# Rows of a convolution kernel: four row bands of TensorE at once, evicted by ScalarE and turned by the store

## The chip, the cores and the metric

The kernel runs on one core of one Trainium2 chip. A core has five engines with instruction queues of their own: TensorE (PE in the profile; its weight loads are shown apart, as PEld), VectorE (DVE), ScalarE (ACT), GpSimd (POOL) and SyncE (SP), which issues most DMAs. The metric is the time of one execution on the device in microseconds; the median of the runs counts.

## The reference

Four layers act on x of 2048 rows by 512 columns (S and D). Layer A filters a normalised x in the two-dimensional frequency domain; layer B convolves each column of a normalised x with a kernel of its own, as long as the sequence, made from a state space of 128 complex states per column. Each adds its result to x, in the order A, B, A, B, with the same weights in both rounds.

```python
def _A_ref(x, w_r, w_i):
    X = rfft2(x, axes=(-2, -1)) * (w_r + 1j * w_i)
    return irfft2(X, s=(S, D), axes=(-2, -1))

def _B_ref(u, A_re, A_im, B_re, B_im, C_re, C_im, log_dt, Dskip):
    dt = exp(log_dt)[:, None]
    logdA, dB = dt * (A_re + 1j * A_im), dt * (B_re + 1j * B_im)
    P = exp(logdA[:, :, None] * arange(L)[None, None, :])
    K = einsum("dn,dnl,dn->dl", C_re + 1j * C_im, P, dB).real
    y = irfft2(rfft2(pad(u.T)) * rfft2(pad(K)))[..., :L]     # along the sequence
    return y.T + u * Dskip

x = x + _A_ref(layernorm(x), ...)
x = x + _B_ref(layernorm(x), ...)
x = x + _A_ref(layernorm(x), ...)
x = x + _B_ref(layernorm(x), ...)
```

What the change touches is on the way from the parameters to the spectrum of K, layer B's kernel. K does not depend on x, is worked out once and serves both rounds.

## The kernel before, in words

**Stages.** The program has four stages: layer A together with all the work on K; layer B; layer A again; layer B again. The Fourier transforms are matmuls with tables, in two steps each, in 32-bit floats.

**K in the first stage.** K is built in eight batches b of 64 columns. Of a batch, six evictions with Exp (exp_k, L1013) and four units (unit_k: L1027 to L1068) make the powers of the states and multiply them out; the unit's matmuls are L1059, their result is copied to a tile KS by L1068. Then rows_k (L1071) takes the first step of K's transform. On the 128 partitions of KS lie four bands of 32 rows, each with 16 of the batch's 64 columns. A matmul of a band takes 32 rows of the table Rk as weights (32 x 128) and 32 rows of KS as the moving side (512 elements), into one PSUM bank of all 128 partitions; a band needs two that add up (h = 0, 1). So there are eight matmuls a batch, each of them two records in the profile, which appear as L1086 with the tile 32*128. Two bands (j = 0, 1) share a PSUM tile of two banks; a = 0, 1 counts these pairs. After each pair's four matmuls DVE empties the tile with a transpose in blocks of 32x32 (L1090) into half of the tile T, and after both SP stores T, 128 rows of 8 KB, to the scratch yk in DRAM (L1093).

**Who reads yk.** In the second stage step_b loads pieces of yk (L813), after all eight batches are stored; L797 multiplies them with the table Gb, ScalarE copies the spectrum out (L819) and it is kept in DRAM as khat for the last stage. The tables Gb and Ib (L769, L770) lie where T and other tiles of the first stage were, so they are loaded after the last store of T has finished; on SP the loads of yk stand behind them. Also needed is layer B's own input: the normalised x (norm_b, L502), its rows (forward_b, matmul L786 and DVE's transpose L789).

**Beside it in the first stage** run layer A's pieces: forward_a (L543 to L551), first_a (fold L564, L664 to L705, with DVE at L673 to L681), inv_a (matmuls L721 and L730, copies L725 and L733, POOL L738 to L746, DVE L741 to L751, and the statistics L479 and L480 for the next norm).

**The order of the work.** A list scheduler in the kernel (Clock) writes the program out while it is built. Every piece of work is a generator; each `yield` names the engines, tiles and PSUM tiles that the next step needs. The scheduler holds a clock for each engine and a price list (fixed part, price per element) and takes, among the steps that can start soonest, the one of lowest rank. rows_k has rank 0. The price of a matmul depends on the shape of its weights. Each engine then executes its instructions in the order written.

**Tiles.** Work tiles come from rings of fixed places: T has one place, KS two, the tables of first_a (G) five. PSUM tiles of kind a, each two banks, are three; the Exp evictions, the units, first_a and rows_k share them.

Of the kernel before, what the change touches and what calls it, by code (L numbers as in the profile page):

```python
# [169 lines left out]
class Clock:  # L170
# [81 lines left out]
    def note(self, ready):  # L252
# [3 lines left out]
        for ins in listed[self.n:]:  # L256
# [7 lines left out]
            start = self.free.get(engine, 0.0)  # L264
            for name, box, w in boxes:
                for other, t, v, by in self.seen.get(name, ()):
                    if (w or v) and t > start and (w != v or box[0][2] > 1) and engine != by and self.meet(box, other):
                        start = t
            out = ins.outs[0].bass_ap
            n = max(int(np.prod([b for _, b in a.ap[1:]])) for a, _ in aps)  # L270
            fixed, each, hop = COST[engine]
# [5 lines left out]
            else:  # L277
                if engine == "PE":
                    n = int(np.prod([b for _, b in out.ap[1:]]))
                    stat, rows = aps[1][0], out.ap[0][1]  # L280
                    if aps[0][0].dtype == BF:
                        each *= 0.25
                    elif rows < 128 and stat.ap[0][1] < 128:
                        each *= max(rows, 32) * stat.ap[0][1] / 16384
                    elif rows < 128:
                        fixed, each = fixed + (0.015 if rows > 32 else -0.005), each * max(rows, 32) / 128
                    elif stat.ap[0][1] < 128:
                        fixed, each = fixed + 0.03, each * max(stat.ap[0][1], 64) / 128
                    elif stat.ap[-1][0] > 2:
                        each *= 2  # L290
                    form = rows, stat.ap[0][1]
# [6 lines left out]
                elif engine == "DVE":  # L298
# [3 lines left out]
                    if ins.opcode == "Reciprocal":  # L302
                        each = 6.3
# [74 lines left out]
class Net:  # L378
# [692 lines left out]
    def rows_k(self, b, KS):  # L1071

        nc = self.nc
        yield "POOL", self.after("kernel", 4 * b + 4)
        o = KS[b][:, 1, :, 0]
        nc.gpsimd.tensor_tensor(o, o, self.Dk[:, 16 * b:16 * b + 16], op=OP.add)
        K = KS[b].rearrange("p h d s -> p h (d s)")
        for a in range(2):
            yield "PE p:a" if a else "PE p:a T"
            if a == 0:  # L1080
                T = self.w("T", [128, 32, 64])
            p = self.psum("a")
            for h in range(2):
                for j in range(2):
                    o = slice(64 * a + 32 * j, 64 * a + 32 * j + 32)
                    nc.tensor.matmul(p[:, 512 * j:512 * j + 512], self.Rk[o, h, :], K[o, h, :], start=h == 0, stop=h == 1)  # L1086
            if a:
                self.drop(KS[b])
            yield "DVE"
            nc.vector.transpose(T[:, :, 32 * a:32 * a + 32].rearrange("p k d -> p d k"), p.rearrange("p (d s) -> p d s", s=32))  # L1090
            self.drop(p)
        yield "SP"
        nc.sync.dma_start(self.yk[b], T.rearrange("p k d -> p (k d)"))  # L1093
        self.mark("rows_k")

    def plan_k(self):
# [173 lines left out]
```

## Time and profile before

Three runs took 852.89 us (median), 852.57 and 856.74. The profiled execution is one of its own:

| | |
|---|---|
| profiled execution | 864.48 us |
| its span, first to last instruction | 862.7 us |
| mean granted clock of TensorE | 0.873 |
| instructions | 20721 |
| busy: PE, PEld | 611.4 us (71%), 369.6 us (43%) |
| busy: DVE, ACT, POOL | 629.9 us (73%), 416.0 us (48%), 361.5 us (42%) |
| L1086, first and last start | 122.0 and 381.2 us |
| first matmul of layer B (L786), first on yk (L797) | 392.36 and 406.72 us |
| DMA | 40132 packets, 82.02 MB, mean 95 GB/s |

Busy time of an engine is a mean over stages that have different limits; the prediction's table of stretches divides it. In a row of a group stand line, engine, operation, tiles, shapes and count, then busy time and the mean ns of one, then the idle time of the engine just before these instructions and what ended it. In a row of a timeline stand start, length, engine, line, operation, shapes and count, and in brackets the wait. Matmuls overlap, so the length of a group of matmuls says more than that of one.

### The profile page before, as it was taken

The numbers are of one execution on the slowest core, as the hardware profiler recorded it, in microseconds if no ns is written. First come the engines' busy times: TensorE is split into PE (matmuls) and PEld (weight loads), VectorE is DVE, ScalarE is ACT, GpSimd is POOL, SyncE is SP. The second block draws the span as 40 slices with busy tenths as digits, with TensorE's granted clock in tenths as the row PEclk, the third lists the DMA queues.
The fourth block names the chain that finished last, engine by engine and source line by source line (L and its number), as shares of the span: only waits on it lengthen the run. The fifth ranks groups of instructions, "written<-read, shape, count | busy, mean of one in ns | idle before, by whom it ended". The sixth has DMA issues, their size and how long they took to land. (4 is left out here: it accounts for less than half of the span.)

```text
span 862.7 us, 20721 instructions
## 1 busy us (share of the span) xinstructions
PE 611.4 (71%) x8808; PEld 369.6 (43%) x8808; DVE 629.9 (73%) x894; ACT 416.0 (48%) x721; POOL 361.5 (42%) x331
## 2 busy tenths in 40 slices
PE   0048689888999778656887874398787863787843
PEld 0037445656667434321444330297675431343410
DVE  6988776965868888976555847776755897756863
ACT  1447686877677866651333330284442553132310
POOL 0037742734537557730334230283432772343510
PEclk9999778999999969857999976599987996997975
DMA  9434003323230601015554312303540003232325
GB/s 235 118 127 122 13 14 130 104 81 104 81 122 26 199 35 51 2 50 206 205 178 149 124 51 80 121 2 127 197 148 1 3 1 146 75 100 75 59 41 97
DMA packets 40132, 82.02 MB, mean 95 GB/s; under 512 B 3465, under 2 KB 21257, under 8 KB 38633
## 3 DMA queue, kind: packets, MB, share of 16 engines
q1 hardware_dynamic: 37736, 72.32, 27.0%
q10 hardware_dynamic: 2304, 8.39, 2.4%
q8 instruction: 69, 1.13, 0.6%
q14 instruction: 23, 0.18, 0.1%
HBM read 57.75 MB, written 22.94 MB: 94 GB/s over the span
## 5 line engine op out<-in xcount | busy, mean ns | idle before, releaser
L837 POOL TENSOR_TENSOR wk<-wk 128x1024 f32<-128x1024 f32 x32 | 75.6, 2366 | 164.0 <-ACT wk L833 164.0
L1046 POOL TENSOR_TENSOR Y<-wk,Y 128x1024 f32<-128x1024 f32 x32 | 77.0, 2407 | 49.7 <-ACT wk L1032 27.7
L845 PE MATMUL ps<-wk 32*64 32x256 f32 x2048 | 76.2, 412 | 18.8 <-POOL wk L837 11.3
L543 PE MATMUL ps<-cRa,wk 128*128 128x128 f32 x128 | 27.7, 301 | 65.7 <-POOL wk L528 65.7
L528 POOL TENSOR_TENSOR wk<-wk 128x256 f32<-128x256 f32 x32 | 25.4, 795 | 101.0 <-DVE wk L504 55.3
L845 PEld LDWEIGHTS ps<-wk 32*64 32x64 f32 x2048 | 43.9, 139 | 53.3 <-POOL wk L837 19.8
L830 DVE TENSOR_TENSOR wk<-ps,wk 128x1024 f32<-128x1024 f32 x32 | 39.0, 1229 | 28.0 <-PE ps L797 18.8
L833 ACT COPY wk<-ps 128x512 f32<-128x512 f32 x32 | 18.8, 586 | 81.6 <-DVE wk L830 81.6
L789 DVE STREAM_TRANSPOSE Y<-ps 128x1024 f32<-128x1024 f32 x24 | 43.6, 1902 | 16.1 <-PE ps L786 16.1
L997 PE MATMUL ps<-wk,Y 96*128 96x512 bf16 x128 | 44.5, 425 | 14.4 <-DVE Y L1040 10.0
L1090 DVE STREAM_TRANSPOSE wk<-ps 128x1024 f32<-128x1024 f32 x16 | 31.6, 1973 | 31.1 <-PE ps L1086 13.8
L1059 PE MATMUL ps<-Y 128*32 128x64 f32 x2048 | 42.3, 245 | 15.0 <-POOL Y L1047 5.7
L1029 DVE SCALAR_TENSOR_TENSOR wk<-wk,ps 128x1024 f32<-128x1024 f32 x32 | 38.8, 1212 | 17.3 <-ACT wk L1027 17.1
L543 PEld LDWEIGHTS ps<-cRa,wk 128*128 128x128 f32 x128 | 21.8, 211 | 68.5 <-POOL wk L528 67.6
L1013 ACT ACTIVATE Y<-ps 128x1024 f32<-128x1024 f32 x48 | 46.7, 1040 | 7.4 <-PE ps L997 7.3
L730 PE MATMUL ps<-wk,cRaT 128*128 128x512 f32 x64 | 38.9, 700 | 15.4 <-ACT wk L725 10.1
L1059 PEld LDWEIGHTS ps<-Y 128*32 128x32 f32 x2048 | 37.0, 126 | 24.8 <-POOL Y L1047 13.1
L1040 DVE TENSOR_TENSOR Y<-ps,Y 128x1024 f32<-128x1024 f32 x32 | 38.9, 1216 | 7.6 <-ACT ps L1033 7.3
L851 ACT COPY Y<-ps 128x512 f32<-128x512 f32 x48 | 25.8, 591 | 36.3 <-PE ps L845 36.3
L862 DVE STREAM_TRANSPOSE Ya<-Y 128x1024 f32<-128x1024 f32 x16 | 35.9, 2267 | 9.9 <-ACT Y L851 9.9
L1047 POOL TENSOR_TENSOR Y<-wk,Y 128x512 f32<-128x512 f32 x32 | 42.4, 1324 | 0.0
L1032 ACT ACTIVATE wk<-wk,quarter 128x1024 f32<-128x1024 f32 x32 | 36.7, 1148 | 10.8 <-DVE wk L1030 10.6
(222 smaller groups left out, 1765.3 us busy)
## 6 DMA issues: line engine op xcount, KB each, us to landing
yk<-wk SPq DMA_DIRECT2D x8, 1024.0 KB
wk<-yk SPq DMA_DIRECT2D x16, 512.0 KB
khat<-wk ACTq DMA_DIRECT2D x16, 512.0 KB
wk<-khat SPq DMA_DIRECT2D x16, 512.0 KB
Y<-in_W_dram SPq DMA_DIRECT2D x12, 515.0 KB
x<-in_cPa_dram SPq DMA_DIRECT2D x16, 384.0 KB
Y<-in_cGa_dram SPq DMA_DIRECT2D x12, 384.0 KB
x<-in_W_dram SPq DMA_DIRECT2D x16, 258.0 KB
```

The costliest lines, as they stand in the source:

```text
L543: nc.tensor.matmul(o, pq[:, 0, :], self.Ra, start=True, stop=False)
L730: nc.tensor.matmul(q, self.RaT, Y4, start=True, stop=True)
L789: nc.vector.transpose(self.P[r][e][:, :, o:o + 32].rearrange("p k d -> p d k"), p.rearrange("p (s d) -> p d s", s=32))
L830: nc.vector.tensor_tensor(t0, X[:, :, 0, None, :].to_broadcast(four), kh, op=OP.mult)
L837: nc.gpsimd.tensor_tensor(t1, xi[:, :, None, :].to_broadcast(four), kh[:, :, ::-1, :], op=OP.mult)
L845: nc.tensor.matmul(v[i // 2][64 * a:64 * a + 64, 512 * (i % 2):512 * (i % 2) + 256], self.Ib[o, g, a, b, :], t[o, a, c, :], start=n == 0, ...
L997: self.nc.tensor.matmul(p, f[:, c:c + 128], self.oh[:k, o:o + 512], start=True, stop=True)
L1013: nc.scalar.activation(m[:, :, 1024:] if i == 2 else m[:, i, :1024], p.rearrange("p (i m) -> p i m", i=2) if i == 2 else p, AF.Exp)
L1040: nc.vector.tensor_tensor(E[:, 1, :1024], p, m[:, :1024], op=OP.mult)
L1046: nc.gpsimd.tensor_tensor(E[:, 0, :1024], c, m[:, :1024], op=OP.mult)
L1047: nc.gpsimd.tensor_tensor(rows(E[:, 0, 1024:]), back(c[:, 512:]), rows(m[:, 1024:]), op=OP.mult)
L1059: nc.tensor.matmul(pk[32 * j:32 * j + 32, 64 * e:64 * e + 64], E1[:, r, i, :], E2[:, r, i], start=r == 0, stop=r == 1)
```

## The change

rows_k issues all eight matmuls of a batch in one step, with the four bands side by side: it takes two PSUM tiles of kind a at once, four banks, and goes through the four bands for h = 0 and then for h = 1. The two tiles are emptied by ScalarE copies and not by DVE's transposes; a copy reads PSUM with a step of 32 elements, so that T holds, on partition k of a block of 32, the elements s by d where the transpose put partition s with k by d. The store takes over the exchange of k and s: four DMAs, each for a block of 32 partitions, which write pieces of 64 elements (256 bytes). The scratch yk has the same contents as before. In the scheduler's price list the price of a matmul with fewer than 128 weight rows and 128 columns changes: a smaller fixed part, and a price that falls down to 32 rows and not only to 64.

```diff
--- before.py
+++ after.py
@@ -285,7 +285,7 @@
                     elif rows < 128:
                         fixed, each = fixed + (0.015 if rows > 32 else -0.005), each * max(rows, 32) / 128
                     elif stat.ap[0][1] < 128:
-                        fixed, each = fixed + 0.03, each * max(stat.ap[0][1], 64) / 128
+                        fixed, each = fixed + 0.01, each * max(stat.ap[0][1], 32) / 128
                     elif stat.ap[-1][0] > 2:
                         each *= 2
                     form = rows, stat.ap[0][1]
@@ -1075,22 +1075,22 @@
         o = KS[b][:, 1, :, 0]
         nc.gpsimd.tensor_tensor(o, o, self.Dk[:, 16 * b:16 * b + 16], op=OP.add)
         K = KS[b].rearrange("p h d s -> p h (d s)")
-        for a in range(2):
-            yield "PE p:a" if a else "PE p:a T"
-            if a == 0:
-                T = self.w("T", [128, 32, 64])
-            p = self.psum("a")
-            for h in range(2):
+        yield "PE p:a p:a T"
+        T = self.w("T", [128, 32, 64])
+        ps = [self.psum("a") for _ in range(2)]
+        for h in range(2):
+            for a in range(2):
                 for j in range(2):
                     o = slice(64 * a + 32 * j, 64 * a + 32 * j + 32)
-                    nc.tensor.matmul(p[:, 512 * j:512 * j + 512], self.Rk[o, h, :], K[o, h, :], start=h == 0, stop=h == 1)
-            if a:
-                self.drop(KS[b])
-            yield "DVE"
-            nc.vector.transpose(T[:, :, 32 * a:32 * a + 32].rearrange("p k d -> p d k"), p.rearrange("p (d s) -> p d s", s=32))
-            self.drop(p)
+                    nc.tensor.matmul(ps[a][:, 512 * j:512 * j + 512], self.Rk[o, h, :], K[o, h, :], start=h == 0, stop=h == 1)
+        self.drop(KS[b])
+        for a in range(2):
+            yield "ACT"
+            nc.scalar.copy(T[:, :, 32 * a:32 * a + 32], ps[a].rearrange("p (d s) -> p s d", s=32))
+            self.drop(ps[a])
         yield "SP"
-        nc.sync.dma_start(self.yk[b], T.rearrange("p k d -> p (k d)"))
+        for q in range(4):
+            nc.sync.dma_start(self.yk[b, 32 * q:32 * q + 32].rearrange("s (k d) -> k s d", k=32), T[32 * q:32 * q + 32])
         self.mark("rows_k")
 
     def plan_k(self):
```

In the changed kernel the matmul is L1085, the copy L1089, and the store keeps L1093. The scheduler, with these steps and prices, writes the first stage in another order; from the first matmul of layer B (L786) on, every engine's order is as it was.

TensorE in the first stage, around the first batch's rows (L1086 and L1085). Before, the two groups of the batch with other work between and behind them:

```order
L1059 MATMUL ps<-Y 32x64 x32
L1086 MATMUL ps<-wk,cRk 128x512 x4
L997 LDWEIGHTS Y
L997 MATMUL ps<-wk,Y 128x512
L997 LDWEIGHTS wk
L997 MATMUL ps<-wk 128x512
L1059 MATMUL ps<-Y 32x64 x32
L1086 MATMUL ps<-wk,cRk 128x512 x4
```

And with the change:

```order
L694 MATMUL ps<-x 64x128
L695 MATMUL ps<-x 64x128
L1085 MATMUL ps<-wk,cRk 128x512 x8
L698 MATMUL ps<-x 128x128
L699 MATMUL ps<-x 128x128
L701 MATMUL ps<-x 128x128
```

The two groups of four are one group of eight, and it stands later, amid the work of first_a.

ScalarE around the second batch's rows, with the change (L1013 is the Exp of the next batch, L1068 the copies of the units, L1089 the new copies):

```order
L1013 ACT_TABLE_LOAD
L1013 ACTIVATE Y<-ps 128x1024
L1068 COPY wk<-ps 128x2x128
L1013 ACTIVATE Y<-ps 128x1024
L1013 ACTIVATE Y<-ps 128x2x512
L1013 ACTIVATE Y<-ps 128x1024 x2
L1068 COPY wk<-ps 128x2x128
L1089 COPY wk<-ps 128x32x32 x2
L705 COPY Ya<-ps 128x4x16x8
L1013 ACTIVATE Y<-ps 128x2x512
```

The pair of copies stands between the fifth and the sixth Exp of a batch, where before ScalarE had only the Exps, a copy of a unit and one of first_a.

DVE at the end of the first stage. Before, from the last reciprocal but one of a norm:

```order
L489 RECIPROCAL rs<-rs 128x4
L492 SCALAR_TENSOR_TENSOR nb<-mv,rs 128x4
L1090 STREAM_TRANSPOSE wk<-ps 128x32x32
L750 TENSOR_TENSOR x<-x,wk 128x256
L751 TENSOR_TENSOR x<-x,wk 128x256
L1090 STREAM_TRANSPOSE wk<-ps 128x32x32
L479 BN_STATS st<-x 128x6
L480 BN_AGGR mv<-st 128x2
```

And with the change:

```order
L489 RECIPROCAL rs<-rs 128x4
L492 SCALAR_TENSOR_TENSOR nb<-mv,rs 128x4
L750 TENSOR_TENSOR x<-x,wk 128x256
L751 TENSOR_TENSOR x<-x,wk 128x256
L741 TENSOR_TENSOR wk<-wk 128x127
L742 TENSOR_TENSOR wk<-wk 128x127
L479 BN_STATS st<-x 128x6
L480 BN_AGGR mv<-st 128x2
```

The two transposes of the last batch are gone from DVE; the additions of inv_a and the statistics follow one another.

## The prediction

> **What bounds the kernel now.** I read the page first, then busy time by stretch, then the waits, and then the timelines around the changed lines. The page's chain reaches back only to 634 us, behind everything the change touches, so it gives no bound here. The touched work, the rows of layer B's kernel (eight batches b), runs from 122 to 393 us in the first stage. Three stretches of it by engine:
>
> ```profile
> core 0: us, PE busy (x) PEld busy (x) DVE busy (x) ACT busy (x) POOL busy (x), PEclk, DMA share, GB/s
> 122.00:300.00 178.00, 162.90 (x2291) 108.90 (x2284) 135.55 (x162) 131.69 (x175) 91.89 (x69) 0.96 0.30 101
> 300.00:372.00 72.00, 50.23 (x828) 27.10 (x828) 66.60 (x103) 48.62 (x76) 49.44 (x50) 0.80 0.09 35
> 372.00:393.00 21.00, 10.14 (x20) 3.36 (x22) 10.62 (x25) 10.56 (x19) 5.59 (x8) 0.50 0.31 117
> ```
>
> From 122 to 300 (six batches) TensorE is busy 162.9 of 178 us, 92%; DVE 76%, ScalarE 74%. From 300 to 372 (one batch) DVE is busy 93%. From 372 to 393 (the last batch) no engine is full: a chain runs through them at a granted clock of 0.50. So the same edit is worth something else in each stretch. The changed work itself:
>
> ```profile
> L1086 PE MATMUL ps<-wk,cRk 32*128 32x512 f32 x128 | 36.9, 700 | 3.7 <-ACT wk L1068 1.9 <-DVE wk L1090 1.6
> L1090 DVE STREAM_TRANSPOSE wk<-ps 128x1024 f32<-128x1024 f32 x16 | 31.6, 1973 | 31.1 <-PE ps L1086 13.8 <-ACT Y L1013 11.8 <-ACT wk L655 5.5
> 122.00:300.00 178.00, 25.39 (x96) 8.50 (x96) 0.96 0.30 101
> ```
>
> The first two rows are groups by line between 60 and 400 us; the third is L1086 alone (PE, PEld) in the first stretch. DVE sat idle 31.1 us just before its 16 transposes: it came to them early and waited. So in the first stretch their 31.6 us are not time that the end depends on; TensorE's 25.4 us there are.
>
> **The change, part by part.**
>
> *Matmuls.* Eight matmuls of a batch went out in two groups of four, two 32-row bands each; now all eight go out together, one band after the other.
>
> ```profile
> 138.07 1.99 PE L1086 MATMUL ps<-wk,cRk 32*128 32x512 f32 x8
> 334.74 1.98 PE L730 MATMUL ps<-wk,cRaT 128*128 128x512 f32 x4
> 421.13 2.18 PE L845 MATMUL ps<-wk 32*64 32x256 f32 x64
> 372.71 3.78 PE L1086 MATMUL ps<-wk,cRk 32*128 32x512 f32 x8 [1.74 <-ACT wk L1068]
> 376.42 2.08 PE L730 MATMUL ps<-wk,cRaT 128*128 128x512 f32 x2
> 378.43 3.78 PE L1086 MATMUL ps<-wk,cRk 32*128 32x512 f32 x8
> ```
>
> These are timeline rows (start, length). A matmul is two records. On the whole array four records of 512 columns take 1.98 us; in L1086 eight take 1.99, so two bands run side by side. L845 uses four bands and two column halves in four banks: 64 records of half the columns, 2.18 us, 34 ns each against 248 ns for L1086's twice as long records. That is over three times as many at once, so four bands do run together. A batch should then cost one group of 1.99 us and not two: half of 25.39, 12.7 us, in the first stretch.
>
> *Evictions.* Gone are 16 DVE transposes of 1.97 us. New are 16 ScalarE copies of 128x1024 out of PSUM that read with a step of 32 elements. No row shows such a read. The nearest:
>
> ```profile
> 407.96 1.01 ACT L819 COPY wk<-ps 128x1024 f32<-128x1024 f32 x1 [15.66 <-PE ps L797]
> L725 ACT COPY wk<-ps 128x512 f32<-128x512 f32 x16 | 9.3, 590 | 2.0 <-PE ps L721 1.9
> L705 ACT COPY Ya<-ps 128x512 f32<-128x512 f32 x12 | 7.1, 589 | 10.8 <-PE ps L702 10.8
> 138.93 4.69 ACT L1013 ACTIVATE Y<-ps 128x1024 f32<-128x1024 f32 x5
> PEld ps L1086 <- DVE wk L1090: 3.1, 5, 1.5
> ```
>
> Low bound 1.01 us (same shape, straight); high bound 1.97, what DVE pays for regrouping the same tile. L705, which writes in pieces of eight, costs what the straight L725 costs, so I take 1.02. In the first stretch ScalarE gains 12 x 1.02 = 12.2 us, 131.7 to 144, still under TensorE's 162.9 - 12.7 = 150.2. But the Exp evictions of a batch run back to back (L1013), and the new order puts the pair of copies among them: there ScalarE is the one waited for. Of the 12.7 us I count **8**; bounds 0 (ScalarE pays all back) and 16 (all, and the 3.1 us that TensorE waited for L1090 from 122 to 300, last row).
>
> The Trainium skill, "TensorEngine Tiling (Array Packing)", section "PSUM Bottleneck", speaks against the change: tiling speeds TensorE up but not the emptying of PSUM, which may become the bottleneck, and both ScalarE and VectorE should empty it. By that the first stretch would gain nothing, and the sum below would be 8 us less; no row before shows it.
>
> *300 to 372.* One batch. DVE loses 2 x 2.0 us where it is 93% busy: I count **3.5**; bounds 1 and 6 (with TensorE's 2).
>
> *372 to 393.* The end of the last batch, by engine:
>
> ```profile
> 376.54 1.91 DVE L1090 STREAM_TRANSPOSE wk<-ps 128x1024 f32<-128x1024 f32 x1 [1.51 <-PE ps L1086]
> 382.26 1.90 DVE L1090 STREAM_TRANSPOSE wk<-ps 128x1024 f32<-128x1024 f32 x1 [3.23 <-PE ps L1086]
> 378.61 0.59 ACT L733 COPY wk<-ps 128x512 f32<-128x512 f32 x1 [2.13 <-PE ps L730]
> 380.16 2.49 POOL L746 TENSOR_TENSOR x<-x,wk 128x512 f32<-128x512 f32 x2
> 384.02 0.63 DVE L479 BATCH_NORM_STATS2 st<-x 128x6 f32<-128x512 f32 x1
> 386.23 0.42 DVE L750 TENSOR_TENSOR x<-x,wk 128x256 f32<-128x256 f32 x1
> 389.38 2.93 ACT L502 ACTIVATE Y<-x,nb,rs 128x512 f32<-128x512 f32 x4 [0.44 <-DVE nb L492]
> 392.36 3.78 PE L786 MATMUL ps<-Y,cRb 64*128 64x512 f32 x8 [10.14 <-ACT Y L502]
> 406.72 1.10 PE L797 MATMUL ps<-wk 64*32 64x256 f32 x32 [0.58 <-DVE Y L789]
> ```
>
> DVE waits 3.23 us for the second group and then transposes 1.9 us, and behind that stand the last statistics, the last normalisation (389.38) and the first matmul of layer B (392.36). Without the transposes DVE's rest depends on L730 alone, which ends at 378.5, then on ScalarE's L733 to 379.2 and on POOL's two L746 to 382.65: the last L750 starts there and not at 386.23, 3.6 us earlier, and the first statistics no longer wait at all. I count **4** earlier for 392.36, and so for L797, 14.36 us behind it.
>
> *The stores.* The same 1 MB a batch, as one DMA with 144 packets before; now the turning is done by four DMAs in pieces of 256 bytes, 4096 a batch.
>
> ```profile
> q1 hardware_dynamic: 144, 1.05, 50.3%
> q1 hardware_dynamic: 8320, 4.19, 35.4%
> 385.00:387.40 2.40, 0.00 (x0) 0.00 (x0) 2.40 (x9) 0.00 (x0) 0.00 (x0) 0.50 1.05 437
> 389.00:398.00 9.00, 5.22 (x12) 1.69 (x12) 3.83 (x5) 2.93 (x4) 0.00 (x0) 0.55 0.99 370
> 384.18 0.32 SPq L1093 DMA_DIRECT2D yk<-wk  x1
> 132.78 0.34 SPq L1093 DMA_DIRECT2D yk<-wk  x1
> 146.38 0.33 SPq L1093 DMA_DIRECT2D yk<-wk  x1
> 388.21 0.33 SPq L769 DMA_DIRECT2D wk<-in_cGb_dram  x1
> SPq L646 <- PE ps L702: 59.8, 9, 15.2
> SPq L1093 <- DVE wk L1090: 126.5, 7, 49.6
> L878 SPq DMA_DIRECT2D out_dram<-x x8: 596/664/2667, 803.2 to 854.9; - x8
> ```
>
> The old store moved in 2.4 us (385 to 387.4, DMA share 1.05). For the new ones the nearest row is the output, written in pieces of 512 bytes from 800 to 862 us: 8320 packets took 35.4% of 16 engines over 62 us, 351 us, 42.2 ns a packet. Bounds for 256 bytes: 21 ns (half the bytes) and 84 ns (a second access a packet); I take 42: 4096 x 42.2 / 16 = **10.8 us a batch**. SP issues four at about 0.66 us (L878's median) in place of one; behind them on SP and in its queue stand loads of tables and of later batches. The stores were 13.6 us apart at the closest (132.78 and 146.38) and up to 50; SP mostly waited, for the tile (126.5 us) and for a free one of the five table buffers (59.8), so its loads run ahead of their use and I cost the delay at 0. Without that cover each load behind a store would come up to 8 us late, once a batch. The tile T has one buffer, free again 10.8 us later, well before the next batch.
>
> After the last batch nothing hides it: SP's L769 waits for the store, then 2.5 MB of tables and the first 0.5 MB of yk go ahead of L797. The last group now ends at 372.71 + 3.78 = 376.5; its copies, with L733 between them, at about 380.2; the packets run from 381 to 391.8; L769 goes at 392.6, 4.4 us later than now. 3 MB at 370 GB/s are 8.1 us, with 0.8 us ahead and 0.8 behind: 402.3. L797 is wanted at 406.72 - 4 = 402.7, so the store just fits: **0**.
>
> The edit in the planner's price of a matmul only moves rows of the first stage; I take no gain from it.
>
> **Sum.** 8 + 3.5 + 4 = 15.5 us. The profiled execution, span 862.7 us (864.48 with what lies around it), becomes about 847; the median run is 11.6 us shorter than it, so 852.9 - 15.5 = 837.4, said as **838 us**.
>
> **The rivals.**
>
> 1. *DVE is the bound throughout.* All 31.6 us of transposes come out of the end: 821 us. For it: 93% in 300 to 372. Against it: the idle time ahead of L1090.
> 2. *Small packets are dear.* At 84 ns a batch's store takes 21.6 us and ends at 402.6; L797 starts at about 413 and not at 402.7. The sum falls to 15.5 - 10.3 = 5, 848 us. The Trainium skill, "DMA: Bandwidth & Descriptors", section "Specifications", says just this: below 512 bytes the DMA reads, modifies and writes; no run so far shows a store below 512.
> 3. *Four bands do not run side by side*, or PSUM's three pairs of banks, two of which a batch now holds at once, stall other work: TensorE gains nothing in the first stretch, 7.5 us remain, 845 us. Against it: L845.
> 4. *Slower: ScalarE takes TensorE's place.* If the stepped read costs 1.97 us, a batch adds 3.9 us to ScalarE and takes 2.1 from TensorE. In the first stretch ScalarE reaches 131.7 + 23.6 = 155, and if its part is the one waited for in every batch, as in the Exp stretch, 6 x 1.9 = 11 us are lost there; the last copies come 2 us later and with them L797, so the tail's 4 fall to 2, and 3.5 to 1.5: 852.9 + 11 - 3.5 = 860 us. It decides from a copy of about 1.6 us on.
>
> **How the numbers follow.** Forecast 0.52 (829 to 846), rival 1 0.05, rival 2 0.16, rival 3 0.12, rival 4 0.15. Two plans of one kernel with hundreds of rows in another order can differ by a few us for no single reason, which is in these widths. The range 826 to 855 reaches over rivals 2 and 3 and leaves out most of 1 and 4, about 2 in 10. About 0.5% (4.3 us) is what a measurement of this kernel can tell from no change: faster means below 848.6. Forecast, rival 1 and most of 3, and a good third of 2, lie below: 0.73. Same takes the rest of 2 and a bit of 3 and 4: 0.12. Slower 0.15.
>
> **What would show it.** Right: L1085 as sixteen records in about 2 us at full clock; copies at L1089 near 1.02 us; the stretch from the first batch to 300 us shorter by some 8 us with TensorE still above 90%; the last batch's stores moving for about 11 us, and L797 waiting on DVE's L789 and not on a DMA. Wrong: sixteen records in 4 us (rival 3), copies near 2 us (rival 4), or an idle TensorE ahead of the first L797 (rival 2). Behind L797 the order of the work is the same, and its length should be too, within 1 us.

## The result, and the profile after

The changed kernel takes 862.99 us (median of 19 runs, 856.93 to 867.79), the kernel before 859.18 us in the runs beside it (19, 851.54 to 866.23). The ratio is **1.0078, interval 1.0053 to 1.0103**: 0.8% slower, where 838 us and "faster" were forecast. This ratio leaves out the slow executions of the kernel before, four that are over 1.5% above its fastest; the two medians over all runs stand at 1.0044. The three runs that the forecast started from (852.89) were themselves at the low end of what this kernel shows.

Its profiled execution took 866.73 us, span 864.9. First the changed work, as groups by line between 60 and 400 us, and the end of the first stage in rows of the timeline:

```profile
L1085 PE MATMUL ps<-wk,cRk 32*128 32x512 f32 x128 | 17.8, 668 | 1.9 <-ACT wk L1068 1.9
L1089 ACT COPY wk<-ps 128x1024 f32<-128x1024 f32 x16 | 15.5, 1013 | 12.3 <-PE ps L1085 12.3
```

```profile
383.12 2.00 PE L1085 MATMUL ps<-wk,cRk 32*128 32x512 f32 x16 [1.87 <-ACT wk L1068]
388.58 4.03 SPq L1093 DMA_DIRECT2D yk<-wk  x4
396.63 0.36 SPq L769 DMA_DIRECT2D wk<-in_cGb_dram  x1
397.00 3.78 PE L786 MATMUL ps<-Y,cRb 64*128 64x512 f32 x8 [10.82 <-ACT Y L502]
411.84 0.45 PE L797 MATMUL ps<-wk 64*32 64x256 f32 x8 [0.59 <-DVE Y L789]
```

A batch's sixteen records take 2.00 us here where two groups took 1.99 us each at full clock; the line's busy time fell from 36.9 to 17.8 us. The copies cost 1.013 us each, and DVE's 31.6 us of transposes are gone. L797 waits for DVE's L789 and for no transfer. Matmuls and copies come out at the forecast size, and yet L786 starts at 397.00 and not at 392.36. The same stretches after (columns as in the prediction's table):

```profile
122.00:300.00 178.00, 152.45 (x2155) 104.83 (x2148) 117.04 (x145) 136.13 (x175) 90.07 (x63) 0.89 0.28 82
300.00:372.00 72.00, 52.47 (x916) 28.91 (x908) 59.80 (x88) 49.53 (x77) 48.56 (x50) 0.81 0.30 82
372.00:393.00 21.00, 9.06 (x118) 4.00 (x118) 19.80 (x36) 16.37 (x29) 11.56 (x13) 0.82 0.10 27
```

From 122 to 300 us TensorE is busy 152.45 us (162.90 before): it idles 25.5 us and not 15.1, at a granted clock of 0.89 and not 0.96. How far the work had come is read from the last start of a line. Before, and then after (instructions, durations in ns, first and last start):

```profile
L705 ACT COPY Ya<-ps x12: 572/586/654, 178.1 to 283.0; 128x512 f32<-128x512 f32 x12
L1068 ACT COPY wk<-ps x32: 357/372/414, 93.2 to 372.3; 128x256 f32<-128x256 f32 x32
```

```profile
L705 ACT COPY Ya<-ps x12: 571/580/607, 174.9 to 296.3; 128x512 f32<-128x512 f32 x12
L1068 ACT COPY wk<-ps x32: 350/372/420, 93.5 to 382.7; 128x256 f32<-128x256 f32 x32
```

first_a ends 13.3 us later and the last unit of K 10.4 us later. From that unit to the first L786 it is 14.3 us (397.0 - 382.7) and not 20.1: the tail gained 5.8. It would be natural to put the loss before 300 us, where first_a falls behind. One of the experiments below speaks against it: p8_a does the changed work in another order and is as fast as the kernel before (1.0001). Its rows:

```profile
L705 ACT COPY Ya<-ps x12: 572/583/607, 174.9 to 296.8; 128x512 f32<-128x512 f32 x12
L1068 ACT COPY wk<-ps x32: 349/372/407, 93.5 to 377.1; 128x256 f32<-128x256 f32 x32
```

There first_a ends as late as in the changed kernel (296.8 and 296.3), but the last unit comes 5.6 us earlier, and L786 starts at 390.8. So what parts the changed kernel from an order of the same work that loses nothing lies behind 300 us. One place stands out, in the seventh batch. TensorE, then the DVE step that it waits for, in the changed kernel:

```profile
321.94 2.46 PE L997 MATMUL ps<-wk,Y 96*128 96x512 bf16 x5 [4.96 <-DVE Y L1040]
320.67 1.21 DVE L1040 TENSOR_TENSOR Y<-ps,Y 128x1024 f32<-128x1024 f32 x1
```

And in p8_a:

```profile
320.06 0.38 PE L997 MATMUL ps<-wk,Y 96*128 96x512 bf16 x1 [2.45 <-DVE Y L1040]
318.79 1.21 DVE L1040 TENSOR_TENSOR Y<-ps,Y 128x1024 f32<-128x1024 f32 x1
```

In the changed kernel's order four of inv_a's L741 and L742 stand on DVE directly ahead of L1040, in p8_a's two. TensorE idles 4.96 us for it and not 2.45, and its granted clock from 317.5 to 324.5 us is 0.50 and not 0.76. (These are single executions; flat_store and serial_in_new, below, have the changed kernel's order and show the same wait, 4.97 and 4.96 us.)

The waits between 122 and 300 us, after and then before (total, times, longest):

```profile
DVE wk L1029 <- ACT wk L1027: 25.2, 4, 11.7
DVE x L673 <- PE ps L665: 15.3, 2, 10.5
ACT wk L1089 <- PE ps L1085: 11.0, 6, 2.6
```

```profile
DVE wk L1029 <- ACT wk L1027: 6.4, 3, 5.4
```

DVE now stands still for up to 11.7 us at a time: 25.2 us for the first step of a unit (L1027), 15.3 for first_a. The forecast's own table had DVE idle 31.1 us ahead of its transposes. With these gone, DVE idles 61.0 us of this stretch and not 42.5 (178 less its busy time). p8_a has such waits too (22.7 us for L1027, 15.3 for first_a), so they don't tell a slower order from an equal one. Two kinds of cause are left: the changed work costs something that the rows above don't show, or the order that the scheduler wrote for it is a worse one.

### The profile page after: what moved, and what is told of

It reads as the page before. It is cut to its first block, busy times and chain, and to the rows that moved or that the text cites. A ratio compares the mean times of both kernels' runs of the same rounds, so it can differ in the third digit from the quotient of the medians.

```text
span 864.9 us, 20745 instructions
## 1 busy us (share of the span) xinstructions
PE 600.6 (69%) x8808; PEld 365.5 (42%) x8808; DVE 614.0 (71%) x878; ACT 429.4 (50%) x737; POOL 364.9 (42%) x331
## 5 line engine op out<-in xcount | busy, mean ns | idle before, releaser
L997 PE MATMUL ps<-wk,Y 96*128 96x512 bf16 x128 | 47.1, 450 | 23.3 <-DVE Y L1040 16.8
L789 DVE STREAM_TRANSPOSE Y<-ps 128x1024 f32<-128x1024 f32 x24 | 43.8, 1905 | 16.4 <-PE ps L786 16.4
L730 PE MATMUL ps<-wk,cRaT 128*128 128x512 f32 x64 | 40.8, 737 | 16.5 <-ACT wk L725 14.0
L1013 ACT ACTIVATE Y<-ps 128x1024 f32<-128x1024 f32 x48 | 47.1, 1037 | 6.8 <-PE ps L997 6.5
L1032 ACT ACTIVATE wk<-wk,quarter 128x1024 f32<-128x1024 f32 x32 | 36.8, 1149 | 19.4 <-DVE wk L1030 19.3
L1040 DVE TENSOR_TENSOR Y<-ps,Y 128x1024 f32<-128x1024 f32 x32 | 38.8, 1212 | 10.0 <-ACT ps L1033 10.0
L1047 POOL TENSOR_TENSOR Y<-wk,Y 128x512 f32<-128x512 f32 x32 | 44.6, 1395 | 0.0
L746 POOL TENSOR_TENSOR x<-x,wk 128x512 f32<-128x512 f32 x32 | 42.4, 1339 | 0.4
```

The lines of the kernel that those rows point to most:

```text
L730: nc.tensor.matmul(q, self.RaT, Y4, start=True, stop=True)
L746: nc.gpsimd.tensor_tensor(xs.rearrange("p (a b) -> p a b", a=2), xs.rearrange("p (a b) -> p a b", a=2), e.rearrange("p a b -> p (a b)")[:, ...
L789: nc.vector.transpose(self.P[r][e][:, :, o:o + 32].rearrange("p k d -> p d k"), p.rearrange("p (s d) -> p d s", s=32))
L997: self.nc.tensor.matmul(p, f[:, c:c + 128], self.oh[:k, o:o + 512], start=True, stop=True)
L1013: nc.scalar.activation(m[:, :, 1024:] if i == 2 else m[:, i, :1024], p.rearrange("p (i m) -> p i m", i=2) if i == 2 else p, AF.Exp)
L1047: nc.gpsimd.tensor_tensor(rows(E[:, 0, 1024:]), back(c[:, 512:]), rows(m[:, 1024:]), op=OP.mult)
```

## The experiments

To part work from order, some kernels follow a fixed order in the first stage: a list of the pieces in the sequence in which the scheduler took them in another kernel replaces its choice. In the diffs below, pick() takes the next piece of that list:

```diff
-            t, p = min((e for e in ready if e[0] <= now), key=lambda e: e[1][:2])
+            t, p = pick(self, ready) or min((e for e in ready if e[0] <= now), key=lambda e: e[1][:2])
```

All ratios are to the kernel before, in runs beside it on the same chip. Its median there lay between 856.77 and 860.75 us, so kernels are compared by their ratios and not by their times.

**New work in the old order (new_in_old_early).** The changed kernel with the order list of the kernel before: the eight matmuls at the place of a batch's first group, the copies at the places of the transposes.

> The changed work (eight matmuls at once, ScalarE copies, stores in 256-byte pieces) in the order of steps that the kernel before has: the eight matmuls stand at the place of the first group of four, the copies at the places of the two transposes, everything else in the first stage stands as before. Theory 1 (the list scheduler's new order bunches the first stage; the changed work itself is cheaper): faster than the kernel before by 6 to 15 us (ratio 0.983 to 0.993), TensorE idle between 122 and 300 us as before (about 15 us), L797 starting 5 us or more before 406.7. Theory 2 (two of three PSUM tile pairs held at once starve the other work): no faster than before, new waits of first_a, the units or the Exp matmuls for a PSUM tile that L1089 frees. Theory 3 (ScalarE's copies land where ScalarE is the one waited for): 0 to 12 us slower than before. Theory 4 (small packets hold up loads): slower or equal, with SP's loads of tables late.

865.12 us, ratio 1.011 (1.0068 to 1.0153): slower, and not faster as theory 1 had it. Of theory 2's sign, waits for a tile that L1089 frees, the trace has one, 2.2 us in all. The timeline shows where; TensorE, then ScalarE, around the second batch:

```profile
138.28 1.89 PE L997 MATMUL ps<-wk,Y 96*128 96x512 bf16 x4
140.10 4.82 PE L1085 MATMUL ps<-wk,cRk 32*128 32x512 f32 x16
144.86 1.04 PE L997 MATMUL ps<-wk,Y 96*128 96x512 bf16 x4
```

```profile
140.10 1.94 ACT L1013 ACTIVATE Y<-ps 128x1024 f32<-128x1024 f32 x2
143.93 1.01 ACT L1089 COPY wk<-ps 128x1024 f32<-128x1024 f32 x1 [1.89 <-PE ps L1085]
145.50 2.85 ACT L1013 ACTIVATE Y<-ps 128x1024 f32<-128x1024 f32 x3 [0.56 <-PE ps L997]
```

The eight matmuls stand in the middle of the L997 that feed the Exps, and take 4.82 us here, at a granted clock of 0.51. ScalarE's third Exp starts at 145.50; before, five ran in one row from 138.93. Behind this place the trace keeps its lag. ScalarE before, and then here:

```profile
157.82 0.41 ACT L1068 COPY wk<-ps 128x256 f32<-128x256 f32 x1
178.14 0.59 ACT L705 COPY Ya<-ps 128x512 f32<-128x512 f32 x1 [1.98 <-PE ps L702]
```

```profile
161.59 0.41 ACT L1068 COPY wk<-ps 128x256 f32<-128x256 f32 x1
181.93 0.58 ACT L705 COPY Ya<-ps 128x512 f32<-128x512 f32 x1
```

3.77 us late at 157.82, 3.79 us late at 178.14: the pace between is the same. (The expectation of the late place, below, says "over the next three batches", which is too much: the rows show it for these 20 us, less than a batch.)

**Old work in the new order (old_in_new).** The kernel before with the order list of the changed one.

> The work of the kernel before (two groups of four matmuls, DVE transposes, one store) in the order of steps that the changed kernel has: both groups stand at the place of the eight matmuls, the transposes at the places of the copies. Theory 1 (order): as slow as the changed kernel or slower, 4 to 15 us over the kernel before. Theories 2 to 4 (the changed work itself costs): within 2 us of the kernel before, or faster than the changed kernel.

882.87 us, ratio **1.0298** (1.0242 to 1.0354): 25.5 us, more than the 4 to 15 that theory 1 expected. The places in the expectation are not exact: the first group stands at the place of the eight matmuls with its transpose directly behind, the second group at the place of the first copy, its transpose at that of the second. With that reservation: in the changed kernel's order the old work is 2.2% slower than the new, 19 us. The new work is the better one there, and the order is the worse one.

**The price alone (price_new).** The kernel before with one line of the change:

```diff
-                        fixed, each = fixed + 0.03, each * max(stat.ap[0][1], 64) / 128
+                        fixed, each = fixed + 0.01, each * max(stat.ap[0][1], 32) / 128
```

> The kernel before with the edit of the price list alone (0.01 and 32 in place of 0.03 and 64); the work itself is unchanged, only the scheduler's order of the first stage moves. If the order's part of the loss comes from the price: 4 to 12 us slower than before. If the price does nothing: within 2 us.

876.95 us, ratio **1.0246** (1.0194 to 1.0297). Not one instruction of the work differs; the order alone costs 21 us, where 4 to 12 were expected.

**Large packets (flat_store).** The changed kernel in its own order. The store leaves out the exchange of k and s, so what is written to yk stands in another order:

```diff
-            nc.sync.dma_start(self.yk[b, 32 * q:32 * q + 32].rearrange("s (k d) -> k s d", k=32), T[32 * q:32 * q + 32])
+            nc.sync.dma_start(self.yk[b, 32 * q:32 * q + 32], T[32 * q:32 * q + 32].rearrange("p k d -> p (k d)"))
```

> The changed kernel in its own order, but the four stores of a batch write whole rows of 8 KB and not pieces of 256 bytes: the exchange of two indices that the store does is left out, so the scratch holds them in another order. Theory 4 (small packets hold up the loads of tables, or the last stores the tables of layer B): 4 us or more faster than the changed kernel. Theories 1 to 3: within 2 us of the changed kernel.

864.3 us, ratio 1.0087 (1.005 to 1.0124), as the changed kernel. Theory 4 falls: the small pieces cost nothing that these intervals, 0.4% wide to either side, could show.

**The late place (new_in_old_late).** As new_in_old_early, with the eight matmuls at the place of the second group and both copies at that of the second transpose.

> The changed work in the order of the kernel before, but with the eight matmuls at the place of the second group of four and both copies at the place of the second transpose. The same work at the place of the first group was 1.1% slower than the kernel before: there the second batch's eight matmuls stand ahead of the matmuls that feed its Exps, and the trace falls back by 3.8 us at this one place and keeps that lag, to within 0.1 us, over the next three batches. Theory of place (a chain through several engines in program order sets the pace; what counts is where the matmuls stand, not how long TensorE is busy): 3 to 7 us faster than the early place, so 858 to 862. Theory of the changed work (PSUM pairs, ScalarE, stores cost wherever they stand): as slow as the early place, 863 to 867. Theory of the prediction (TensorE's freed time comes out): 845 or less.

863.46 us, ratio 1.0025 (0.9991 to 1.0059). The place is worth 0.85% (1.011 to 1.0025), some 7 us, as the theory of place expected. (By the time alone, 863.46 us would count for the theory of the changed work; but the kernel before took 860.75 us beside this kernel and 857.06 beside the early one.) Both kernels do the same work on every engine. The prediction's gain isn't there either.

**Evictions and stores alone (act_only).** The kernel before, its order, two groups of four:

```diff
-            yield "DVE"
-            nc.vector.transpose(T[:, :, 32 * a:32 * a + 32].rearrange("p k d -> p d k"), p.rearrange("p (d s) -> p d s", s=32))
+            yield "ACT"
+            nc.scalar.copy(T[:, :, 32 * a:32 * a + 32], p.rearrange("p (d s) -> p s d", s=32))
...
-        nc.sync.dma_start(self.yk[b], T.rearrange("p k d -> p (k d)"))
+        for q in range(4):
+            nc.sync.dma_start(self.yk[b, 32 * q:32 * q + 32].rearrange("s (k d) -> k s d", k=32), T[32 * q:32 * q + 32])
```

> The kernel before with the evictions and the stores alone changed: two groups of four matmuls as before, at their places, ScalarE copies at the places of the two transposes, four stores in 256-byte pieces. TensorE's order is the same as before, row for row. If ScalarE's copies land where ScalarE is waited for: 3 to 12 us slower than before. If neither DVE's 31.6 us nor ScalarE's 16 us lie on the chain: within 2 us of before. If DVE's time comes out as predicted for 300 to 393 us: 4 to 7 us faster.

863.13 us, ratio 1.0034 (1.0004 to 1.0065): about 3 us slower, and not 4 to 7 us faster by DVE's time. In one batch the timeline shows what a place on ScalarE can cost, before and then here:

```profile
327.92 1.99 PE L1086 MATMUL ps<-wk,cRk 32*128 32x512 f32 x8 [0.28 <-DVE wk L1090]
```

```profile
330.21 1.00 ACT L1090 COPY wk<-ps 128x1024 f32<-128x1024 f32 x1
331.27 3.78 PE L1086 MATMUL ps<-wk,cRk 32*128 32x512 f32 x8 [2.40 <-ACT wk L1090]
```

The first group's copy stands on ScalarE behind a table load and two steps of a unit (L1032, L1033), and the second group waits 2.40 us for the tile; then it takes 3.78 us and not 1.99, at a granted clock of 0.50. Before, it waited 0.28 us for DVE's transpose.

**The changed work at the old price (price_old).** The price line above, reversed, in the changed kernel.

> The changed kernel with the old price of the matmul (0.03 and 64), so that the scheduler plans the changed work at the price it had before. The kernel before with the new price was 2.5% slower. If the new price makes worse orders in general: 8 to 20 us faster than the changed kernel, 843 to 855. If an order is a draw that the price only reshuffles: anywhere between 850 and 880, on either side of the changed kernel.

863.04 us, ratio 1.0022 (0.999 to 1.0055). The old price is not what was missing: 843 to 855 did not come. The other expectation, 850 to 880, came, but nearly any time would have met it.

**A small step of the price (nudge1).** The kernel before with 0.025 in place of 0.03.

> The kernel before with a slightly other price of the same matmuls (fixed part 0.025 in place of 0.03, no other edit): the work is the same, the scheduler writes the first stage in another order. If an order is a draw and the kernel before holds a good one: 4 to 20 us slower. If only the changed price (0.01 and 32) makes bad orders: within 3 us of before.

869.92 us, ratio 1.0095 (1.006 to 1.013). An edit of 5 ns in a price list, with no change of the work, costs 8 us.

**One loop exchanged (serial_in_new).** The changed kernel, its order:

```diff
-        for h in range(2):
-            for a in range(2):
+        for a in range(2):
+            for h in range(2):
```

> The changed kernel in its own order, with one loop exchanged: the eight matmuls go through the two bands of a = 0 and then the two of a = 1, as before, instead of through all four bands. Everything else (two PSUM tiles at once, ScalarE copies, small stores) stays. In the changed kernel's order the old work was some 20 us slower than the new. If that gain is TensorE's (the prediction's term): a batch's eight matmuls take 3 to 4 us in place of 2, and the kernel is 6 to 14 us slower than the changed one. If TensorE's time is off the chain: within 2 us of the changed kernel, TensorE just idles less.

862.71 us, ratio 1.0057 (1.0027 to 1.0088), as the changed kernel. It does not test TensorE's term, because its premise fell:

```profile
140.14 2.01 PE L1085 MATMUL ps<-wk,cRk 32*128 32x512 f32 x16
```

Issued two bands at a time, the eight matmuls still take 2.01 us.

**DVE back (dve_in_new).** The changed kernel in its own order, eight matmuls at once, with DVE's transposes at the places of the copies and the old store (act_only's diff, reversed).

> The changed kernel in its own order, with the evictions and the store as before: DVE transposes at the places of ScalarE's copies, one store of 8-KB rows; the eight matmuls through four bands stay. If the gain of the new work over the old in this order is DVE's: 8 to 20 us slower than the changed kernel. If DVE's transposes stand in its idle time: within 3 us of the changed kernel, or faster, as ScalarE loses 16 us of copies.

869.95 us, ratio 1.016 (1.0115 to 1.0205), 0.8% above the changed kernel: about 7 us, a little under the 8 to 20 of the first expectation. In this order the evictions on ScalarE are a gain, though DVE's transposes (30.0 us) still come after 30.3 us of idle time:

```profile
L1089 DVE STREAM_TRANSPOSE wk<-ps 128x1024 f32<-128x1024 f32 x16 | 30.0, 1939 | 30.3 <-issue 16.1 <-PE ps L1085 12.4 <-ACT wk L655 1.9
```

**Four bands, old evictions, old order (bands_old_late).** The same work as dve_in_new in the order of the kernel before, all of it at the second group's and the second transpose's place.

> In the order of the kernel before: the eight matmuls through four bands at the place of the second group, both DVE transposes at the place of the second transpose, the old store. TensorE loses half of its time in these matmuls and nothing else changes but the places. The prediction's term for this alone: 8 us faster than before (range 0 to 12.7). The theory that chains in program order set the pace: within 3 us of before.

875.72 us, ratio **1.0227** (1.0168 to 1.0286): 19 us slower, though a batch's matmuls go out at once; neither expectation came. With ScalarE's copies at the same places (new_in_old_late) it was 1.0025, so evicting with the two transposes together at one place, 4 us in a row on DVE, costs 17 us more there.

**The same step for the changed work (nudge_a).** The changed kernel with 0.025 and 64.

> The changed kernel with the price of the matmul at 0.025 and 64, the same small step away from 0.03 and 64 that made the kernel before 1% slower. If an order is a draw: another time than with 0.03 and 64 (863.0), by up to 10 us on either side. If the changed work's time does not depend on the draw: within 3 us of it.

863.66 us, ratio 1.0073 (1.0046 to 1.01). The order turned out the same as price_old's on TensorE, DVE and GpSimd, with a few rows of ScalarE apart. So it is in effect a repeat: two comparisons of one kernel, on two chips, gave 1.0022 and 1.0073. Half a per cent is what one of these ratios is good for.

**TensorE's term by itself (twice_in_new).** The changed kernel in its own order, the eight matmuls issued twice:

```diff
+        for _ in range(2):
             for h in range(2):
                 for a in range(2):
                     for j in range(2):
```

> The changed kernel in its own order, with the eight matmuls of a batch issued twice (the second pass overwrites the first with the same sums): TensorE gets the 2 us a batch back that the change saved, 12.7 us from 122 to 300 us and about 4 us behind, and no other engine's work changes. If TensorE's time there is on the path (the prediction's term of 8): 6 to 12 us slower than the changed kernel (869 to 875). If it is hidden behind the chain through ScalarE, DVE and GpSimd: within 3 us of it.

879.79 us, ratio **1.023** (1.0183 to 1.0277), 1.5% above the changed kernel: 13 us, give or take 5, at or over the upper end of what was expected.

```profile
L1086 PE MATMUL ps<-wk,cRk 32*128 32x512 f32 x256 | 33.4, 656 | 2.7 <-ACT wk L1068 2.7
L1090 ACT COPY wk<-ps 128x1024 f32<-128x1024 f32 x16 | 15.5, 1015 | 26.8 <-PE ps L1086 26.8
```

(In this kernel the lines are one further on.) TensorE got 33.4 - 17.8 = 15.6 us more to do, and 13 of them came out at the end; ScalarE's wait ahead of the copies rose from 12.3 to 26.8. So in this order time added to these matmuls is on the path, nearly in full.

**More orders of both works (nudge2, mid_b, p8_a, mid_a, q5_a).** nudge2 is the kernel before with 0.035 and 64, mid_b with 0.02 and 48; p8_a is the changed kernel with 0.03 and 32, mid_a with 0.02 and 48, q5_a with 0.02 and 40.

> The kernel before with the fixed part of that matmul's price at 0.035 in place of 0.03: the same work in another order of the first stage. If the order of the kernel before is a lucky draw: 5 to 20 us slower than it, as the two others so far (0.95% and 2.46%). If it is an ordinary one: as often faster as slower, within 5 us.

> The kernel before with that price at 0.02 and 48, one more order of the old work. Lucky draw: 5 to 20 us slower than the kernel before. Ordinary: within 5 us on either side.

> The changed kernel with that price at 0.03 and 32, another order of the changed work (over 400 rows of TensorE differ from either of the two tried). The changed work in four orders stood at 0.2 to 1.1% above the kernel before. If its time hardly depends on the draw: in the same band, 860 to 868. If some order shows the predicted gain: under 850.

> The changed kernel with the price of the matmul at 0.02 and 48, the partner of mid_b (old work, 0.6% above the kernel before). If the changed work gains some 7 us on the old in the middle of the draws: 852 to 862, that is from 0.5% under the kernel before to 0.5% over it. If the pair shows no gain of the work: 863 or more.

> The changed kernel with that price at 0.02 and 40, one more order of the changed work, over 300 rows of TensorE away from each of the others. The same band, 852 to 866; under 852 it would beat both kernels.

All orders that the scheduler itself wrote, ratio to the kernel before and interval:

| price: fixed part, columns | old work | changed work |
|---|---|---|
| 0.03, 64 | 1 (before) | 1.0022 (0.9990 to 1.0055) price_old |
| 0.025, 64 | 1.0095 (1.0060 to 1.0130) nudge1 | 1.0073 (1.0046 to 1.0100) nudge_a, a repeat of price_old |
| 0.035, 64 | 1.0105 (1.0071 to 1.0140) nudge2 | not run |
| 0.02, 48 | 1.0059 (1.0028 to 1.0090) mid_b | 1.0024 (0.9991 to 1.0057) mid_a |
| 0.02, 40 | not run | 1.0119 (1.0056 to 1.0183) q5_a |
| 0.03, 32 | not run | 1.0001 (0.9971 to 1.0030) p8_a |
| 0.01, 32 | 1.0246 (1.0194 to 1.0297) price_new | 1.0078 (1.0053 to 1.0103) after |

The old work was slower in each of its four other orders; the mean of all five is 1.010. The changed work lies between 1.000 and 1.012 in its five orders (price_old and nudge_a counted as one), mean 1.005. At 0.025, at 0.02 and 48, and at 0.01 the changed work is ahead in its row (only at 0.01 by more than one ratio is good for); at 0.03 and 64, where the kernel before stands, it is behind, within its interval. q5_a came out above its band of 852 to 866, p8_a at the lower end of its own. No order beat the kernel before: the best, p8_a and mid_a, are equal to it within their intervals.

The first stretch, for old_in_new, price_new, mid_b and p8_a in turn:

```profile
122.00:300.00 178.00, 152.35 (x1982) 101.49 (x1981) 128.97 (x147) 122.14 (x158) 85.16 (x61) 0.93 0.23 79
```

```profile
122.00:300.00 178.00, 158.08 (x2013) 103.38 (x2009) 126.72 (x150) 122.34 (x158) 83.16 (x60) 0.92 0.24 84
```

```profile
122.00:300.00 178.00, 163.04 (x2286) 108.98 (x2284) 136.91 (x160) 130.89 (x176) 93.12 (x69) 0.96 0.28 94
```

```profile
122.00:300.00 178.00, 151.32 (x2148) 104.11 (x2140) 116.30 (x145) 136.08 (x175) 89.29 (x63) 0.89 0.28 81
```

With the old work, the good orders (before, and mid_b, the next best) have TensorE busy 163 us at 0.96 and some 2290 matmul records done by 300 us; the two bad ones 152 to 158 us at 0.92 or 0.93 and about 2000. nudge1 and nudge2 are like the bad ones (157.79 us, 0.91, 2056 records; 155.28 us, 0.94, 2100). With the changed work this does not part the orders: p8_a and the changed kernel look alike there.

## Why the prediction was wrong

**The step that failed** is, first, its assumption on the order: "Two plans of one kernel with hundreds of rows in another order can differ by a few us for no single reason, which is in these widths", together with "The edit in the planner's price of a matmul only moves rows of the first stage; I take no gain from it". The new order was given a mean of zero and a few us of width. Measured by price_new, nudge1, nudge2, mid_b and old_in_new, the old work takes 5 to 21 us more in four other orders of the scheduler and 25.5 in the changed kernel's. That price edit alone, in the old work, is worth 21 us. The kernel before was not an ordinary starting point but the best of five orders of its work. Whether this is chance, or its prices were chosen with this order in view, no run tells; either way the forecast should have expected a new order to cost something. By the table the mean loss over the four is 1.26%, 11 us.

**A second step failed with it: the gain was read from the rows of one order and taken to hold there.** "Of the 12.7 us I count 8" rests on TensorE being busy 92% of the first stretch. In just that order, that of the kernel before, the new work gains nothing: 1.0025 (0.9991 to 1.0059) with the matmuls at the better place, 1.011 at the other, where the sum of 15.5 us asks for 0.982. By parts: evictions and stores alone lost 3 us there (act_only, 1.0034), where 3.5 + 4 were to be gained, and the grouping of the matmuls on top of them brought nothing that a ratio can tell (1.0034 to 1.0025), where 8 us, 0.9%, were counted. Why TensorE's freed time did not come out in that order stays open; at one place (new_in_old_early) the matmuls delay the Exps.

**In the changed kernel's order the work gains what was forecast, by luck.** There TensorE's 2 us a batch are worth 13 us (twice_in_new, which adds them and does not take them away) and the evictions 7 (dve_in_new); old against new work is 19. The forecast was 15.5 for all, but worked out from rows of the other order, where nothing of it came. The order took 25.5, and what is left, 0.8%, is the result (old_in_new with the reservation on its places).

**122 to 300 us, 8 us.** The forecast took 12.7 us of TensorE and cut it to 8 because ScalarE gets 12.2. In the changed order little had to be cut, as far as the 13 us can tell. "Shorter by some 8 us with TensorE still above 90%" did not come: first_a ended 13.3 us later, TensorE at 86%. p8_a reads the same (151.32 of 178 us busy, 0.89) and equals the kernel before, so this alone is not the loss.

**300 to 372 us, 3.5 us.** Not seen: the last unit came 10.4 us later. From the end of first_a to the last unit the changed kernel takes 86.4 us (382.7 - 296.3) and p8_a 80.3 (377.1 - 296.8); that is where these two part. The kernel before takes 89.3 (372.3 - 283.0), so against it the lag fell from 13.3 to 10.4 in this stretch.

**372 to 393 us, 4 us.** Right in kind; measured 5.8 from the last unit to L786. DVE no longer has transposes between L750 and the statistics, as forecast. But the last matmuls also ran at a granted clock of 1.00, in 2.00 us, where the forecast kept the 3.78 us of the half clock; how much of the 5.8 is this the runs don't part.

**The stores, 0 us.** Right (flat_store), with the packet mis-sized. The last batch's stores are the only traffic from 389 to 396:

```profile
389.00:396.00 7.00, 0.00 (x0) 0.00 (x0) 4.47 (x11) 6.17 (x11) 1.03 (x1) 0.50 0.57 149
```

0.57 of 16 engines over 7.00 us are 64 us for 4096 packets, 15.6 ns each, where 42.2 was taken and 21 was the low bound. The old store of the same 1 MB took 1.05 of 16 engines over 2.40 us, 40 us, so the small pieces do cost the DMA engines more, 1.6 times as much, but not over eight times as at rival 2's 84 ns (344 us). The Trainium skill's rule ("DMA: Bandwidth & Descriptors", section "Specifications": below 512 bytes the DMA reads, modifies and writes) stood beside rival 2. Whether the extra 24 us are its price no run tells; the time of the kernel doesn't show them (flat_store).

**Rivals.** Rival 4 had the right side and nearly the right time (860) for a wrong reason: the stepped copy costs 1.013 us, not 1.97. Rival 3's halves: the four bands do run side by side; that two PSUM tiles held at once stall other work was not tried by itself, but in the trace of the changed kernel no engine waits for L1089, the copies that free them, and the changed work equals the kernel before in two orders with both tiles held. Rival 1, DVE as the bound throughout, falls with the waits above: DVE has less to do and idles more. The Trainium skill's warning ("TensorEngine Tiling (Array Packing)", section "PSUM Bottleneck": the emptying of PSUM may become the bottleneck) does not show in the changed kernel either: nothing waits for the copies there. In act_only a wait of 2.40 us for one of them shows, from its place on ScalarE and not from its 1.00 us.

**Behind L797** the length was to hold within 1 us. From there to the second round's first L786 it was 317.2 us before (723.9 - 406.7) and 314.5 after (726.3 - 411.8), so this missed by 2 us, with no change of the work. In the profiles of six more kernels here (old_in_new, p8_a, mid_a, price_old and the two of new_in_old) it is 312.8 to 316.8 us; the spread belongs to the executions.

**What stays open.** Which property makes an order good is not settled. TensorE's wait for L1040 in the seventh batch goes roughly with the time of the changed work: 4.96 us in the changed kernel and 4.87 in q5_a, the two orders that came out slowest, 1.1 to 2.5 in price_old, mid_a and p8_a. With the old work it does not: mid_b has one of 7.98 us and is the next best. No run moved this one step by itself. From 122 to 300 us a lower granted clock goes with TensorE's idle time in the changed kernel (0.89 against 0.96). The Trainium skill ("TensorE: Matmul & The Clock Gate", section "HAM oscillation — how this bites in real kernels") says that idle gaps between bursts bring the half clock back; the gap of 4.96 us with the clock of 0.50 around it agrees. But p8_a, also at 0.89 from 122 to 300, equals the kernel before, so the clock of this stretch alone does not decide. Whether the price edit harms the changed work (1.0078 against 1.0022 and 1.0073 for the old price) is within what one ratio is good for.

## What to carry to other kernels

Where a scheduler writes the order, an edit changes two things, the work and the order, and the second can be the larger: first measure the old work in a few other orders (a price moved by 5 ns was enough here), and judge the edit against that spread and not against the one tuned order. Whether an engine's time is on the path depends on the order too: the same new work was worth 19 us in one order and nothing in another, so ask it of the order that will run. A group that got shorter in all can still do harm in the middle of a stream that feeds another engine: there the eight matmuls were 7 us worse than at a later place.

## What was not expected of the hardware

- **Bands overlap whichever way they are issued.** Eight matmuls of four 32-row bands take 2.00 us issued across all bands and 2.01 us issued as two bands and then two (serial_in_new). In the kernel before, two groups with other work between them took 1.99 us each. So it is enough that the groups follow each other directly.
- **A stepped PSUM read cost ScalarE nothing.** 128x1024 read with a step of 32 elements: 1.013 us, straight 1.01.
- **Small packets cost less than forecast, their issue more.** 256-byte packets took 15.6 ns each. SP needed 4.03 us for the last batch's four DMAs of 1024 pieces and 0.32 us for one of 128 rows. Most of that is the number of DMAs and not of pieces: four of 32 rows (flat_store) took 2.69 us.

```profile
387.37 2.69 SPq L1093 DMA_DIRECT2D yk<-wk  x4
```
